# Scores of two slots in one row-tiled visit, in a PSUM tile of five banks

## The chip, the cores and the metric

The kernel runs on one core of one Trainium2 chip. The metric is the device time of one execution in microseconds; the median of several runs counts. All data are fp32.

The engines are named as in the profile: PE (TensorE matmuls) with PEld (its weight loads), DVE (VectorE), ACT (ScalarE), POOL (GpSimd) and SP (the queue that issues most DMAs). PSUM is the memory that matmuls write; it has 8 banks, each with room for 512 fp32 values in each of 128 partitions. A matmul of fp32 shows in the trace as two weight loads and two matmul records.

## What is computed

Threshold attention over 8 batches and 8 heads, sequence 576, head size 64, and then a two-layer MLP with GELU over all 4608 rows:

```python
scores = scale * np.matmul(q, k.transpose(0, 1, 3, 2))          # (8, 8, 576, 576)
thresh = np.max(scores, axis=-1, keepdims=True) - tau
scores = np.where(scores >= thresh, scores, -1000000000.0)
attn = np.exp(scores - np.max(scores, axis=-1, keepdims=True))
attn = attn / (np.sum(attn, axis=-1, keepdims=True) + 1e-09)
x = np.matmul(attn, v)                                          # then rearranged to (4608, 512)
h = x @ w_in                                                    # w_in (512, 2048)
out = (0.5 * h * (1.0 + erf(h / sqrt(2)))) @ w_out              # w_out (2048, 512)
```

## The kernel before

The order of all instructions on each engine is written out by hand; the framework adds the semaphores between engines.

**Pairs and slots.** Two heads form a pair, p = 0 to 31; head e = 0 lies in partitions 0 to 63 of the transposed queries (qT) and keys (kT), head e = 1 in partitions 64 to 127. The 576 query rows of a pair are four chunks of 128 (i = 0 to 3) and one of 64, and the 64 last rows of both heads together make chunk i = 4, which is one tile of 128 rows (q_tail). A slot is one (p, i). The first four pairs (p < EARLY) run while weights are loaded and converted; their slots are in another order and their transposes are made on PE. The 28 others run slot after slot.

**One slot.** `scores` (L394) makes the scores of a slot: for every head two matmuls of 288 columns, each half in a bank of its own. For i < 4 the heads use the upper and the lower 64 rows of the PE array at once (row tiling). The scores of each head are a tile `sc` of two banks, and there are two such buffers, four banks in all. `softmax_head` (L406) takes, head by head, the maximum on DVE (L415), the threshold on POOL (L416) and the exponential on ACT (L418), all but the threshold from `sc`. `softmax_tail` (L421) masks and sums on DVE, head by head (L434), and reads `sc` again. After that `turn_p` (L488) transposes the probabilities on DVE (L498), and DMAs regroup them. In slot 2 `turn_qk` (L375) transposes the next pair's queries and keys on DVE, and `weigh_v` (L522) multiplies the previous pair's probabilities with v into two tiles `xT`.

**MLP beside it.** Eight of the eighteen blocks of 256 rows (PLAIN) run between the slots. `fill` (L637) puts in as many matmuls as a table of goals says; `block_steps` (L602) makes hT = w_in.T x (tiles `hT`, L613), then the second product (tiles `o_ps`, L628). The GELU of a finished hT is put off: `gelus(left)` (L573) leaves `left` of them, 0 at the start of a slot, `lag[0]` within `fill` (2 in the later slots). `table` (L596) brings back the exponential's table on ACT.

**The last stage.** The ten last blocks are multiplied by two levels of a Strassen-Winograd scheme (`last_blocks`, L973). `chain` (L828) makes up to seven products m1 to m7 into three PSUM tiles: x (m1, m6, m5), y (m7, m4, m3) and v (m2). After each product `taken` (L809) copies the tile on ACT or adds it into a sum on DVE. m5 and m3 are made in the following chain: `m1, m5 of the chain before, m7, m2, m3 of the chain before, m6, m4`. `layer_in` (L856) has 7 chains with all seven products, `layer_out` (L920) five single products and then 5 chains without m2; each runs eight times.

**PSUM.** The pool `ps` (L80) has tag `sc` with 2 buffers of two banks and tag `mm` with 4 buffers of one bank, for hT, o_ps, xT, the transposes `tr`, and y and v of the last stage. The lines that matter:

```python
ps = ctx.enter_context(tc.tile_pool(name="ps", bufs=4, space=PSUM))
sc = s["sc", i] = [ps.tile([P, 2, 512], FP32, tag="sc", name="sc", bufs=2) for _ in range(n)]
```

Of the kernel before, what the change touches and what calls it, by code (L numbers as in the profile page):

```python
# [8 lines left out]
FP32 = mybir.dt.float32  # L9
# [9 lines left out]
def kernel(  # L19
# [57 lines left out]
    const = ctx.enter_context(tc.tile_pool(name="const", bufs=1))  # L77
    small = ctx.enter_context(tc.tile_pool(name="small", bufs=4))
    dram = ctx.enter_context(tc.tile_pool(name="dram", bufs=1, space=bass.MemoryType.DRAM))
    ps = ctx.enter_context(tc.tile_pool(name="ps", bufs=4, space=PSUM))  # L80

    XSLOTS = 7
    w_in_all = const.tile([P, N_DM, d_ff], FP32, name="w_in")
# [38 lines left out]
    make_identity(nc, ident)  # L122


    q_tail = [att.tile([P, P], FP32, name=f"q_tail{i}") for i in range(4)]
    v_sb = [att.tile([P, 2, KR, D], FP32, name=f"v{i}") for i in range(4)]

# [173 lines left out]
    def turn_qk_early(p):  # L301


        s = st[p]
        if 2 <= p < HP:
            qT = op.tile([P, MAIN], FP32, tag="o_sb", name="qT")
            kT = pd_tail[p - 2].rearrange("p b i -> p (b i)")
        else:
            qT = ld.tile([P, MAIN], FP32, tag="qT", name="qT")
            kT = ld.tile([P, TAIL + S], FP32, tag="kT", name="kT")  # L310
        s["qT"], s["kT"] = qT, kT
        qt = s["q_tail"] = q_tail[p % 4]
        copy = nc.scalar.copy if p else nc.vector.tensor_copy
        for name in "qk":
            t = s[name]
            tr = ps.tile([P, NC, P], FP32, tag="mm", name="tr")
# [8 lines left out]
        tr = ps.tile([P, NC, P], FP32, tag="mm", name="tr")  # L325
# [12 lines left out]

    def turn_p_early(p, i):


        s = st[p]
        if i == 0 or (p < HP and i == 2):
            s["pT"] = [one.tile([P, KR, S], FP32, tag=f"pT{e}", name=f"pT{e}") for e in range(2)]
        w = s.pop(("p", i))
        n = 1 if i == NC else 2

        def turn(to, at):
            nc.tensor.transpose(to, w[:, at:at + P], ident)  # L349

        for e in range(n):
            tr = ps.tile([P, NC, P], FP32, tag="mm", name="tr")
# [9 lines left out]
        tr = ps.tile([P, NC, P], FP32, tag="mm", name="tr")  # L362
# [12 lines left out]
    def turn_qk(p):  # L375
# [7 lines left out]
        qt = s["q_tail"] = q_tail[p % 4]  # L383
        qs, ks = s.pop("q"), s.pop("k")
        nc.vector.transpose(kT.rearrange("p (b i) -> p b i", i=Q), ks)
        nc.vector.transpose(
            qT.rearrange("p (c a i) -> p c a i", c=NC, i=Q),
            qs[:, 0:MAIN // Q, :].rearrange("p (a c) j -> p c a j", c=NC))
# [3 lines left out]
                qt[rows, e * TAIL:(e + 1) * TAIL].rearrange("p (b i) -> p b i", i=Q), qs[rows, MAIN // Q:NB, :])  # L392

    def scores(p, i):  # L394
        s = st[p]
        n = 1 if i == NC else 2
        sc = s["sc", i] = [ps.tile([P, 2, 512], FP32, tag="sc", name="sc", bufs=2) for _ in range(n)]
        for h in range(2):
            for e in range(n):
                rows = slice(0, P) if i == NC else slice(e * D, (e + 1) * D)  # L400
                lhsT = s["q_tail"] if i == NC else s["qT"][rows, i * P:(i + 1) * P]
                at = h * HALF + (TAIL if p < EARLY and e == 0 else 0)
                nc.tensor.matmul(  # L403
                    sc[e][:, h, 0:HALF], lhsT=lhsT, rhs=s["kT"][rows, at:at + HALF], start=True, stop=True)

    def softmax_head(p, i):  # L406

# [3 lines left out]
        thr = s["thr", i] = small.tile([P, 2], FP32, tag="thr", name="thr")  # L411
        w = s["p", i] = work.tile([P, 2 * S], FP32, tag="p", name="p")
        for e in range(n):
            sc = s["sc", i][e][:, :, 0:HALF]
            nc.vector.tensor_reduce(nmx[:, e:e + 1], sc, axis=AXIS.XY, op=ALU.max, negate=True)  # L415
            nc.gpsimd.tensor_scalar(  # L416
                thr[:, e:e + 1], nmx[:, e:e + 1], -1.0, tau_eff, op0=ALU.mult, op1=ALU.subtract)
            nc.scalar.activation(  # L418
                w[:, e * S:(e + 1) * S].rearrange("p (h s) -> p h s", h=2), sc, AF.Exp, bias=nmx[:, e:e + 1], scale=1.0)

    def softmax_tail(p, i):  # L421

# [7 lines left out]
            at = [e * NC + i if i < NC else 2 * NC for e in range(n)]  # L430
            den = [sums[p % 2][:, x:x + 1] for x in at]
        for e in range(n):
            row = w[:, e * S:(e + 1) * S].rearrange("p (h s) -> p h s", h=2)
            nc.vector.scalar_tensor_tensor(  # L434
                row, sc[e][:, :, 0:HALF], thr[:, e:e + 1], row, op0=ALU.is_ge, op1=ALU.mult, accum_out=den[e])
# [9 lines left out]
    def divide_early(p, lo, hi):  # L445
# [1 line left out]

        s = st[p]
        b, hp = divmod(p, HP)
        tr = ps.tile([P, 512], FP32, tag="mm", name="tr")  # L450
# [348 lines left out]
    def product(to, pairs, start):  # L799
        for k, (l, r) in enumerate(pairs):  # L800
            nc.tensor.matmul(to, lhsT=l, rhs=r, start=start and k == 0, stop=k == len(pairs) - 1,  # L801
                             skip_group_check=not start)

    def bank(tag, n):
        if tag == "sc":
            return ps.tile([P, 2, 512], FP32, tag="sc", name="bank", bufs=2)[:, 0, 0:n]
        return ps.tile([P, 512], FP32, tag="mm", name="bank")[:, 0:n]

    def taken(to, x, first):  # L809

# [208 lines left out]
    nc.scalar.activation(warm[:, 1:2], warm[:, 0:1], AF.Exp)  # L1019
    load_early(1)  # L1020
    load_early(2)
    for t in q_tail + v_sb:
        nc.gpsimd.memset(t, 0.0)
    for _ in range(4):
        load_piece(nc.sync)
# [34 lines left out]
    for n in range(len(slots) + WEIGH + 1):  # L1060
# [69 lines left out]
            turn_qk(p + 1)  # L1130
        convert(0 if n == 0 else 1200 if n < 3 else 2200 if n < BATCH - 1 else 1e9)
        if not early:
            lag[0] = 2 if p < NP else 0
            if n != BATCH:
                fill(owed, tokens)
                owed = 0.0
# [49 lines left out]
```

## Time and profile before

| what | value |
|---|---|
| median of 3 runs | 1352.98 us (1352.51 to 1354.1) |
| profiled execution | 1353.51 us, span 1351.4 us |
| granted PE clock, mean | 0.993 |
| sc matmuls, two heads (L403, 64x128 weights, 288 columns) | 960 + 64 records, 175.6 us busy |
| sc matmuls, last rows (L403, 128x128 weights) | 120 + 8 records |
| maximum on DVE (L415) | 288 x 750 ns, 205.4 us |
| exponential on ACT (L418) | 288 x 738 ns, 201.9 us |
| mask and sum on DVE (L434) | 288 x 816 ns, 225.3 us |
| transpose of probabilities on DVE (L498) | 112 x 1378 ns, 154.4 us |
| hT (L613), o_ps (L628) matmuls | 1024 and 512 records, 241.8 and 236.8 us |
| xT matmuls (L537) | 1280 records, 169.3 us |
| sums of the last stage on DVE (L683, 128x320 and 128x256) | 304 x 488 ns, 240 x 420 ns |

Busy times are sums over the span; several engines are busy at once. The mean of one instruction counts from its start to its end, and matmuls overlap in that sense, so their busy time is less than count times mean. In the profile's groups an arrow `out<-in` gives tiles by the program's names with the buffer numbers left out, and `x288` the count. A wait "A <- B" is idle time of engine A that ended when B's instruction did. In timelines, an entry with x8 merges eight neighbours of one kind.

### The profile page before, as it was taken

Reading aid. Unit: us, or ns where it says so; the run is one execution under the profiler, and the core shown is the slowest. Engines: PE = TensorE matmul, PEld = TensorE weight load, DVE = VectorE, ACT = ScalarE, POOL = GpSimd, SP = SyncE. Lnnn points to the kernel's source line nnn. Section 1 sums busy time; section 2 is a strip of 40 time slices with the busy share of each in tenths; the row PEclk is TensorE's granted clock in tenths of the full one; section 3 lists DMA queues with packets and bytes.
Section 4 is the critical chain, followed back from the end, with each engine's and each line's share of the span. In section 5 each row is a group of like instructions: output and inputs, shape, how many; then the busy total and the mean of one; then the engine's idle time right before and its main releaser. Section 6 shows DMA issues by size and latency. Waiting matters only on the chain.

```text
span 1351.4 us, 19821 instructions
## 1 busy us (share of the span) xinstructions
PE 1323.0 (98%) x6282; PEld 893.8 (66%) x6282; DVE 1048.1 (78%) x1997; ACT 605.0 (45%) x1027; POOL 659.0 (49%) x1097
## 2 busy tenths in 40 slices
PE   8799899999999999999999999999999999999998
PEld 6476557467467557557557557568787787877877
DVE  6987677788888888888888888874758698385765
ACT  7876527548547538537638636413201112211120
POOL 5785354555555554554554551144363513635530
PEclk9899999999999999999999999999999999999999
DMA  8642276677777787687687777500000041000003
GB/s 268 187 151 52 58 164 156 146 162 185 155 180 182 161 193 178 160 207 172 153 208 180 155 179 152 117 9 0 1 0 1 14 112 32 0 1 0 1 0 78
DMA packets 209781, 152.39 MB, mean 113 GB/s; under 512 B 113360, under 2 KB 193088, under 8 KB 209680
## 3 DMA queue, kind: packets, MB, share of 16 engines
q1 hardware_dynamic: 188224, 112.53, 37.5%
q0 software_dynamic: 21024, 38.32, 9.9%
q8 instruction: 51, 0.84, 0.3%
q14 instruction: 50, 0.41, 0.1%
q10 hardware_dynamic: 432, 0.30, 0.1%
HBM read 55.97 MB, written 12.52 MB: 51 GB/s over the span
## 4 chain that ended last, share of the span: by engine, by line
PE 93%; DVE 3%; ACT 3%; DMA 1%; issue 1%; SPq 0%; POOL 0%; DVEq 0%; ACTq 0%; POOLq 0%
PE bank L801 34%; PE o_ps L628 17%; PE hT L613 16%; PE sc L403 14%; PE xT L537 11%; ACT p L418 1%; DMA x<-xall 1%; DVE nmx L415 1%; DVE p L434 1%; PE tr L349 1%; ACT pT L356 1%; DVE power L212 0%; ACT power L202 0%; DVE power L210 0%; PE tr L456 0%
## 5 line engine op out<-in xcount | busy, mean ns | idle before, releaser
L418 ACT ACTIVATE p<-sc,nmx 128x576 f32<-128x576 f32 x288 | 201.9, 738 | 284.0 <-DVE nmx L415 283.7
L434 DVE SCALAR_TENSOR_TENSOR p<-sc,thr,p 128x576 f32<-128x576 f32 x288 | 225.3, 816 | 70.1 <-ACT p L418 68.6
L416 POOL TENSOR_SCALAR thr<-nmx,tau_eff 128x1 f32<-128x1 f32 x288 | 88.0, 307 | 368.0 <-DVE nmx L415 355.8
L415 DVE TENSOR_REDUCE nmx<-sc 128x1 f32<-128x576 f32 x288 | 205.4, 750 | 53.5 <-PE sc L403 52.3
L613 PE MATMUL hT<-xall,w_in 128*128 128x256 f32 x1024 | 241.8, 385 | 0.0
L628 PE MATMUL o_ps<-w_out,g 128*128 128x512 f32 x512 | 236.8, 603 | 0.0
L613 PEld LDWEIGHTS hT<-xall,w_in 128*128 128x128 f32 x1024 | 189.4, 190 | 50.0 <-issue 23.0
L683 DVE TENSOR_TENSOR c<-c,bank 128x320 f32<-128x320 f32 x304 | 147.3, 488 | 33.6 <-PE bank L801 20.1
L683 DVE TENSOR_TENSOR o<-o,bank 128x256 f32<-128x256 f32 x240 | 99.8, 420 | 93.7 <-PE bank L801 88.7
L403 PE MATMUL sc<-kT,qT 64*128 64x288 f32 x960 | 161.8, 431 | 9.3 <-DVE p L434 8.6
L537 PE MATMUL xT<-pT,v 128*64 128x256 f32 (+1 forms) x1280 | 169.3, 418 | 0.8 <-DVE pT L360 0.5
L628 PEld LDWEIGHTS o_ps<-w_out,g 128*128 128x128 f32 x512 | 93.1, 190 | 109.1 <-issue 106.8
L498 DVE STREAM_TRANSPOSE turned_p<-p 128x1152 f32<-128x1152 f32 x112 | 154.4, 1378 | 3.9
L403 PEld LDWEIGHTS sc<-kT,qT 64*128 64x128 f32 x960 | 92.4, 187 | 83.8 <-issue 69.7
L537 PEld LDWEIGHTS xT<-pT,v 128*64 128x64 f32 x1280 | 93.0, 140 | 75.4 <-issue 15.1
L801 PE MATMUL bank<-w_out,c 128*128 128x256 f32 x480 | 120.2, 381 | 0.5 <-DVE o L683 0.5
L269 POOL DMA_DIRECT2D v<-in_v_dram x208 | 110.9, 536 | 3.9 <-issue 1.9
L801 PEld LDWEIGHTS bank<-w_out,c 128*128 128x128 f32 x480 | 89.9, 190 | 18.8 <-DVE o L683 3.0
L854 ACT ACTIVATE c<-c 128x320 f32<-128x320 f32 (+1 forms) x80 | 46.9, 623 | 114.6 <-DVE c L683 114.6
L683 POOL TENSOR_TENSOR c<-c,g 128x320 f32<-128x320 f32 (+1 forms) x40 | 50.5, 1271 | 67.4 <-DVE c L683 67.4
L801 PE MATMUL bank<-t_out,c 128*128 128x256 f32 x320 | 82.7, 381 | 0.0
L801 PE MATMUL bank<-t_out,g 128*128 128x256 f32 x320 | 82.1, 379 | 0.0
(179 smaller groups left out, 1775.1 us busy)
## 6 DMA issues: line engine op xcount, KB each, us to landing
pT<-turned_p SPq DMA_DIRECT2D x448, 160.0 KB, 3.6
pT<-pd_tail SPq DMA_DIRECT2D x112, 80.0 KB, 3.0
q<-in_q_dram POOLq DMA_DIRECT2D x104, 72.0 KB, 3.4
k<-in_k_dram POOLq DMA_DIRECT2D x104, 72.0 KB, 3.2
inv<-turned SPq DMA_DIRECT2D x54, 128.0 KB, 3.9
v<-in_v_dram POOLq DMA_DIRECT2D x156, 40.0 KB, 3.1
out_dram<-o SPq DMA_DIRECT2D x40, 128.0 KB, 2.4
xall<-in_moe_w_out_dram POOLq DMA_DIRECT2D x9, 512.0 KB, 3.8
```

Of the source, the lines that this page charges most:

```text
L269: eng.dma_start(t[r:P:4, e, 0:n, :], rows[:, r * KR:r * KR + n, :])
L403: nc.tensor.matmul(sc[e][:, h, 0:HALF], lhsT=lhsT, rhs=s["kT"][rows, at:at + HALF], start=True, stop=True)
L415: nc.vector.tensor_reduce(nmx[:, e:e + 1], sc, axis=AXIS.XY, op=ALU.max, negate=True)
L416: nc.gpsimd.tensor_scalar(thr[:, e:e + 1], nmx[:, e:e + 1], -1.0, tau_eff, op0=ALU.mult, op1=ALU.subtract)
L418: nc.scalar.activation(w[:, e * S:(e + 1) * S].rearrange("p (h s) -> p h s", h=2), sc, AF.Exp, bias=nmx[:, e:e + 1], scale=1.0)
L434: nc.vector.scalar_tensor_tensor(row, sc[e][:, :, 0:HALF], thr[:, e:e + 1], row, op0=ALU.is_ge, op1=ALU.mult, accum_out=den[e])
L498: nc.vector.transpose(turned_p[:, :, i // 2, 0:NB, i % 2 * Q:(i % 2 + 1) * Q], w.rearrange("p (e b i) -> p e b i", e=2, i=Q))
L537: nc.tensor.matmul(to, lhsT=s["v"][:, e, c, :], rhs=rhs, start=(c == 0), stop=(c == KR - 1))
L613: nc.tensor.matmul(hT[:, j % 2, :], lhsT=w_in_sb[c][:, j * P:(j + 1) * P], rhs=x_blk[n][:, c, :], start=(c == 0), stop=(c == N_DM - 1))
L628: nc.tensor.matmul(o[:, 0:d_model], lhsT=g[j][:, m * P:(m + 1) * P], rhs=w_out_sb[j], start=(j == 0), stop=(j == N_DF - 1))
L683: eng.tensor_tensor(out, a, b, op=ALU.add)
L801: nc.tensor.matmul(to, lhsT=l, rhs=r, start=start and k == 0, stop=k == len(pairs) - 1, skip_group_check=not start)
```

## The change

The scores lie in one PSUM tile `sc_all` of five banks. Two slots have a place in it at the same time: slot "pair" 0 has head 0 at columns 0 to 575 and head 1 at 1408 to 1983, "pair" 1 has head 0 at 576 to 1151 and head 1 at 1984 to 2559. Each region crosses one border of banks, so each head's scores are two matmuls of unequal size (512 + 64, 128 + 448, 448 + 128, 64 + 512 columns).

In the 28 later pairs `scores` makes slots 0 and 1 in one visit, 2 and 3 in one, and slot 4 alone; `flip` alternates which slot takes which place. Both row tiles would write bank 2 in such a visit, so the 128 last columns of place 1, head 0 are made first by a matmul over all 128 rows, with both heads' qT as weights and `k_end` as the other operand: the keys of head 0 with zeros for head 1. `turn_qk` copies `k_end` on ACT.

The pool of `mm` has three buffers instead of four. The early transposes and spread tiles take bank 4 of `sc_all` every fourth time, as long as no later slot uses it (`spare_bank`). In the last stage `bank` puts x in banks 0 and 1 of `sc_all` in turn, and y and v in turn in the `mm` pool and in banks 2 to 4. Maximum, exponential and mask read one run of 576 columns instead of two of 288. `lag[0]` in the later slots is 1 instead of 2.

```diff
-    ps = ctx.enter_context(tc.tile_pool(name="ps", bufs=4, space=PSUM))
+    ps = ctx.enter_context(tc.tile_pool(name="ps", bufs=3, space=PSUM))
+    BANK = 512
+    sc_all = ps.tile([P, 5 * BANK], FP32, tag="sc", name="sc", bufs=1)
+    SC_AT = {(0, 0): 0, (1, 0): S, (0, 1): 5 * BANK - 2 * S, (1, 1): 5 * BANK - S}
+    flip = [0]
+    CUT = 2 * BANK - S
+    spare = [0]
+    def spare_bank():
+        spare[0] = (spare[0] + 1) % 4
+        if spare[0] or (EARLY in st and ("sc", 1) in st[EARLY]):
+            return ps.tile([P, BANK], FP32, tag="mm", name="tr")
+        return sc_all[:, 4 * BANK:5 * BANK]
...
+    k_end = att.tile([P, 2 * S - 2 * 512], FP32, name="k_end")
...
+        nc.scalar.copy(k_end[0:D, :], kT[0:D, CUT:S])
...
     def scores(p, i):
         s = st[p]
-        n = 1 if i == NC else 2
-        sc = s["sc", i] = [ps.tile([P, 2, 512], FP32, tag="sc", name="sc", bufs=2) for _ in range(n)]
-        for h in range(2):
-            for e in range(n):
-                rows = slice(0, P) if i == NC else slice(e * D, (e + 1) * D)
-                lhsT = s["q_tail"] if i == NC else s["qT"][rows, i * P:(i + 1) * P]
-                at = h * HALF + (TAIL if p < EARLY and e == 0 else 0)
-                nc.tensor.matmul(
-                    sc[e][:, h, 0:HALF], lhsT=lhsT, rhs=s["kT"][rows, at:at + HALF], start=True, stop=True)
+        if p >= EARLY and i < NC and i % 2:
+            return
+        first = flip[0] if p >= EARLY else 0
+        todo = [i, i + 1] if p >= EARLY and i < NC else [i]
+        parts = []
+        for k, c in enumerate(todo):
+            pair = (first + k) % 2
+            heads = range(1 if c == NC else 2)
+            s["sc", c] = [sc_all[:, SC_AT[pair, e]:SC_AT[pair, e] + S] for e in heads]
+            for e in heads:
+                cut = -SC_AT[pair, e] % BANK or BANK
+                start = 0
+                for lo, hi in (0, cut), (cut, S):
+                    whole = c < NC and pair == 1 and e == 0 and lo == CUT
+                    parts.append((-1 if whole else k, start, e, c, lo, hi))
+                    start += hi - lo
+        for k, _, e, c, lo, hi in sorted(parts):
+            rows = slice(0, P) if c == NC or k < 0 else slice(e * D, (e + 1) * D)
+            lhsT = s["q_tail"] if c == NC else s["qT"][rows, c * P:(c + 1) * P]
+            at = TAIL if p < EARLY and e == 0 else 0
+            rhs = k_end if k < 0 else s["kT"][rows, at + lo:at + hi]
+            nc.tensor.matmul(s["sc", c][e][:, lo:hi], lhsT=lhsT, rhs=rhs, start=True, stop=True)
+        if i == NC and p >= EARLY:
+            flip[0] ^= 1
...
+    turn = {"sc": 0, "mm": 0}
     def bank(tag, n):
-        if tag == "sc":
-            return ps.tile([P, 2, 512], FP32, tag="sc", name="bank", bufs=2)[:, 0, 0:n]
-        return ps.tile([P, 512], FP32, tag="mm", name="bank")[:, 0:n]
+        turn[tag] += 1
+        k = turn[tag] % (2 if tag == "sc" else 6)
+        if tag == "mm" and k % 2:
+            return ps.tile([P, BANK], FP32, tag="mm", name="bank")[:, 0:n]
+        k = k if tag == "sc" else 2 + k // 2
+        return sc_all[:, k * BANK:k * BANK + n]
...
-            lag[0] = 2 if p < NP else 0
+            lag[0] = 1 if p < NP else 0
```

More of the change, by code (lines that the diff above doesn't have):

```diff
@@ L315, in turn_qk_early @@
             t = s[name]
-            tr = ps.tile([P, NC, P], FP32, tag="mm", name="tr")
+            tr = spare_bank().rearrange("p (c s) -> p c s", s=P)
             for c in range(NC):
@@ L324, in turn_qk_early @@
                 copy(kT[:, TAIL:S], src)
-        tr = ps.tile([P, NC, P], FP32, tag="mm", name="tr")
+        tr = spare_bank().rearrange("p (c s) -> p c s", s=P)
         for j, name in enumerate("qk"):
@@ L351, in turn_p_early @@
         for e in range(n):
-            tr = ps.tile([P, NC, P], FP32, tag="mm", name="tr")
+            tr = spare_bank().rearrange("p (c s) -> p c s", s=P)
             for c in range(NC):
@@ L361, in turn_p_early @@
         tails = s["pT"][0][:, NC, :]
-        tr = ps.tile([P, NC, P], FP32, tag="mm", name="tr")
+        tr = spare_bank().rearrange("p (c s) -> p c s", s=P)
         turn(tr[:, 0, :], MAIN if i < NC else S - P)
@@ L413, in softmax_head @@
         for e in range(n):
-            sc = s["sc", i][e][:, :, 0:HALF]
-            nc.vector.tensor_reduce(nmx[:, e:e + 1], sc, axis=AXIS.XY, op=ALU.max, negate=True)
+            sc = s["sc", i][e]
+            nc.vector.tensor_reduce(nmx[:, e:e + 1], sc, axis=AXIS.X, op=ALU.max, negate=True)
             nc.gpsimd.tensor_scalar(
@@ L418, in softmax_head @@
             nc.scalar.activation(
-                w[:, e * S:(e + 1) * S].rearrange("p (h s) -> p h s", h=2), sc, AF.Exp, bias=nmx[:, e:e + 1], scale=1.0)
+                w[:, e * S:(e + 1) * S], sc, AF.Exp, bias=nmx[:, e:e + 1], scale=1.0)
     def softmax_tail(p, i):
@@ L432, in softmax_tail @@
         for e in range(n):
-            row = w[:, e * S:(e + 1) * S].rearrange("p (h s) -> p h s", h=2)
+            row = w[:, e * S:(e + 1) * S]
             nc.vector.scalar_tensor_tensor(
-                row, sc[e][:, :, 0:HALF], thr[:, e:e + 1], row, op0=ALU.is_ge, op1=ALU.mult, accum_out=den[e])
+                row, sc[e], thr[:, e:e + 1], row, op0=ALU.is_ge, op1=ALU.mult, accum_out=den[e])
         if p < EARLY:
@@ L449, in divide_early @@
         b, hp = divmod(p, HP)
-        tr = ps.tile([P, 512], FP32, tag="mm", name="tr")
+        tr = spare_bank()
         for i in range(lo // P, -(-hi // P)):
@@ L1021 @@
     load_early(2)
-    for t in q_tail + v_sb:
+    for t in q_tail + v_sb + [k_end]:
         nc.gpsimd.memset(t, 0.0)
```

## The prediction

> **What bounds the kernel now.** I read the page's engine shares and chain first, then busy time by stage, then who waits for whom in the attention stage, then the timelines of single slots.
>
> ```profile
> PE 1323.0 (98%) x6282; PEld 893.8 (66%) x6282; DVE 1048.1 (78%) x1997; ACT 605.0 (45%) x1027; POOL 659.0 (49%) x1097
> PE 93%; DVE 3%; ACT 3%; DMA 1%; issue 1%; SPq 0%; POOL 0%; DVEq 0%; ACTq 0%; POOLq 0%
> ```
>
> TensorE holds 93% of the chain that ended last. By stage (columns: stretch, its length, then busy us of PE, PEld, DVE, ACT, POOL):
>
> ```profile
> 0.00:138.60 138.60, 120.93 (x814) 87.92 (x815) 104.24 (x205) 102.41 (x210) 91.90 (x146) 0.95 0.55 161
> 138.60:862.00 723.40, 717.54 (x3470) 433.13 (x3471) 608.11 (x1089) 408.49 (x624) 367.59 (x759) 1.00 0.73 165
> 862.00:900.00 38.00, 38.00 (x130) 19.58 (x129) 30.48 (x62) 7.53 (x16) 12.25 (x16) 1.00 0.27 61
> 900.00:1351.00 451.00, 446.52 (x1872) 353.20 (x1871) 305.29 (x644) 86.61 (x178) 187.30 (x176) 1.00 0.07 18
> ```
>
> The second stretch is the 28 later head pairs, 723.4 / 28 = 25.84 us each; VectorE is 84% busy there, so it has little room. The waits of 200 to 860 us (total, times, longest):
>
> ```profile
> DVE p L434 <- ACT p L418: 57.2, 127, 2.5
> DVE nmx L415 <- PE sc L403: 31.1, 54, 2.2
> PE sc L403 <- DVE p L434: 1.6, 2, 1.3
> ```
>
> TensorE loses 1.6 us there to buffers of scores. A one-head slot, then a two-head slot:
>
> ```profile
> 505.25 0.76 DVE L415 TENSOR_REDUCE nmx<-sc 128x1 f32<-128x576 f32 x1
> 506.04 0.74 ACT L418 ACTIVATE p<-sc,nmx 128x576 f32<-128x576 f32 x1 [3.23 <-DVE nmx L415]
> 506.88 0.82 DVE L434 SCALAR_TENSOR_TENSOR p<-sc,thr,p 128x576 f32<-128x576 f32 x1 [0.88 <-ACT p L418]
> ...
> 512.64 1.24 PE L403 MATMUL sc<-kT,qT 64*128 64x288 f32 x8
> 513.81 3.72 PE L613 MATMUL hT<-xall,w_in 128*128 128x256 f32 x16
> ...
> 513.91 1.42 DVE L415 TENSOR_REDUCE nmx<-sc 128x1 f32<-128x576 f32 x2
> 514.79 1.35 ACT L418 ACTIVATE p<-sc,nmx 128x576 f32<-128x576 f32 x2
> 515.62 0.82 DVE L434 SCALAR_TENSOR_TENSOR p<-sc,thr,p 128x576 f32<-128x576 f32 x1 [0.28 <-ACT p L418]
> ```
>
> In a two-head slot head 0's exponential lies beside head 1's maximum: maxima 1.42 together, and from the first maximum to the end of the second mask (517.18) 3.27 us. The one-head slot shows the serial price: maximum to mask 1.63 us. Finally the last stage:
>
> ```profile
> 1012.30 0.70 PE L801 MATMUL bank<-x,s_out 128*128 128x320 f32 x2
> 1012.84 0.70 PE L801 MATMUL bank<-t_x,s_out 128*128 128x320 f32 x2
> ...
> 1012.50 0.49 DVE L683 TENSOR_TENSOR g<-g,bank 128x320 f32<-128x320 f32 x1
> ```
>
> A product takes 0.54 us; the sum that empties it starts 0.2 us after it, lasts 0.49, and runs beside the next products, because each product has a bank tile of its own.
>
> **What the skill says.** "PSUM — Partial Sum Buffer", section on bank collisions: two engines may not be at one bank and quadrant together, and the compiler back end adds a dependency between them, "reads and writes alike". No run here shows a collision; the trace's overlaps are all on different banks. "TensorEngine Tiling (Array Packing)", Key Properties: a change of tiling mode drains TensorE; Gotcha 1: row tiles may not write one bank together. The trace agrees on the first: eight score matmuls stream in about 0.97 us (four steps of 0.243), and hT starts 1.17 after them, with some 0.2 more lost on entry; I take 0.4 us for both switches.
>
> **The premise that decides.** What waits for what is set by the framework that places the semaphores. From small programs built with it: for an SBUF tile it follows regions, but for a PSUM tile it follows the whole tile and lets one engine at it at a time, readers too, even where banks differ. Today two heads' scores, and every product of the last stage, are tiles of their own. The change makes one tile, sc_all, of five banks, for four score regions, a quarter of the early transposes and most accumulators of the last stage. No page states a whole-tile rule and the trace of before cannot show it; the bank rule is the rival below.
>
> **Attention stage, by the premise.** Head 1's maximum waits for head 0's exponential and head 0's mask for head 1's exponential. From first maximum to last mask: 1.63 + 1.63 + 1.56 (both masks, 515.62 to 517.18) = 4.82 instead of 3.27. A visit of TensorE may begin only when the last mask is done and no maximum before the whole visit is done. The visit: 0.1 signal, 0.11 weight load, 0.22 for the full-row piece (two records of 128 columns), 0.2 switch, 2.05 for head 1's pieces (128, 448, 64, 512 columns, two records each, at 0.84 ns a column from hT's 0.215 us per 256, short ones at 0.107, the price of a 128-column weight load in "TensorE: Matmul & The Clock Gate", LDWEIGHTS), 0.19 to the first maximum: 2.87. Slot by slot:
> - slot 0: 4.82 + 0.04 + the transpose of 1.38 (L498) = 6.24
> - slot 1: 4.82 + the visit 2.87 (the transpose lies beside it) = 7.69
> - slot 2: 4.82 + 0.04 + 3.04 (transpose and turn_qk, 522.56 to 525.60) = 7.90
> - slot 3: 4.82 + the one-head visit, full mode, 0.1 + 0.11 + 1.03 + 0.19 = 6.25
> - slot 4: 2.45 (505.25 to 507.70) + 2.87 = 5.32
>
> Sum 33.4 against 25.84: +7.56, times 28 = **+212 us**. TensorE's 24.7 us a pair fit inside, so mode switches saved are worth nothing here. For the same reason three banks instead of four, lag 1 instead of 2 and the k_end copy (64 x 128 on ScalarE, an estimated 0.27 us behind turn_qk's transpose) cost nothing; in the rival where TensorE still bounds they do.
>
> **Early stage.** 16 two-head slots with +1.55 = 25 us; 19 of the 76 early transposed or spread tiles go to bank 4 of sc_all, so TensorE waits for the exponentials and the mask for ScalarE's copy: 1 us each as a middle value (0 to 2), 19. Uneven pieces, 512 + 64 beside 128 + 448: 0.1 each, hidden. **+45** (15 to 75).
>
> **Last stage.** x is always in sc_all; of the others every second one. Where two products on sc_all follow each other, the second waits: 0.2 + 0.49 + 0.06 signal + 0.11 weight load = 0.86 us (0.79 with 256 columns, whose sum takes 0.42); with one other product of 0.54 between, 0.32 is left; with one of 0.86, nothing. The 56 chains of layer_in: one direct and three covered, 0.86 + 0.96 = 1.82, 102 us. The 40 of layer_out: three of five have both accumulators in sc_all (four direct, 3.16), two one (1.58), and v some 1.6 a round: 8 x (3 x 3.16 + 2 x 1.58 + 1.6) = 114. **+216** (150 to 260). That six banks for y and v now stand where four did could win back at most the 4.5 us for which a weight load waits for VectorE.
>
> **Clock.** TensorE would idle some 4 us twice a pair. "TensorE: Matmul & The Clock Gate", Part 1, has the clock halved after an idle window of about 3.4 us; the profile before shows a lower clock only in its first slices (0.95 over 138.6 us). An estimate: a quarter of 56 gaps, 1 us each: **+14** (0 to 60).
>
> **Sum.** The profiled execution took 1353.51 (span 1351.4 and 2.1 around it): 1353.5 + 212 + 45 + 216 + 14 = 1840.5. The median of the runs is 0.5 lower; I forecast 1840.
>
> **Rivals.**
> *Waits by bank, TensorE and VectorE in step.* For: the column layout, built so that heads of one slot share no bank. Then heads overlap as now, but slots share banks 1 to 3, so a visit starts late and the maximum waits for most of it. Worked as above: of six borders in two pairs, three leave VectorE idle for 1.1, 0.7 and 1.1 us; 1.45 a pair, 41 us. Besides, with three banks handed out in order of release the second xT of slot 2 gets the bank of slot 1's hT, whose GELU stands behind slot 2's exponentials (ends 523.41, xT begins about 521.4); some 1.3 us in 13 pairs, partly in the same gaps. About 1400.
> *Faster.* If no read of sc_all waits for another read, and slot 2's regions are free well before TensorE comes, it stays bound by its own work: 56 visits fewer x 0.4 = -22.4; full-row pieces 56 x 0.22 = +12.1; short pieces 56 x 0.1 = +5.6; tails and early pieces +3; last stage -4.5. About 1347. It decides from where VectorE's part of two slots (9 to 10 us) is shorter than TensorE's work up to the next visit (6.9 us from slot 1, so against it).
>
> **How the numbers follow.** Whole-tile waits 0.84, by bank 0.10, faster 0.06. The first case with its bounds gives 1700 to 1970, which holds nearly all of its chance; the others are left out. About 0.2% (2.7 us) is what can be told from no change. The rivals' own spread gives faster 0.05, same 0.02, slower 0.93.
>
> **What would show it.** Right: DVE nmx <- ACT p appears as a large wait in a slot (some 0.9 us per two-head slot); ACT and DVE never at sc together; TensorE near 72% busy; PE bank <- DVE and ACT in the last stage about 200 us; a pair every 33 us. Wrong: the two maxima still within 1.42 us, or last-stage products still 0.54 apart; then waits go by bank or region and a rival holds. Pair period right but last stage too short would mean covered waits there.

## The result and the profile after

The changed kernel takes 1998.64 us (median of 4 runs, 1993.83 to 2002.43) against 1352.82 before: a ratio of 1.477, 95% interval 1.4735 to 1.4804. The forecast of 1840 us had the direction and the kind of loss, and was 159 us short. The profiled execution took 1993.83 us, its span is 1992.1.

One statement about the kernel before has to be put right first, because the largest miss hangs on it. The section on it gives x the products m1, m6, m5 and y the products m7, m4, m3. The last line of `chain` says otherwise, in both kernels:

```python
waiting.append((one_of("m5", x, False), one_of("m3", x, False)))
```

x takes four products (m1, m6, m5 and m3), y two (m7 and m4).

Engine shares and chain of the changed kernel:

```profile
PE 1534.4 (77%) x6282; PEld 916.8 (46%) x6282; DVE 1055.7 (53%) x1997; ACT 634.5 (32%) x1059; POOL 658.3 (33%) x1098
PE 42%; DVE 29%; ACT 10%; SPq 7%; issue 6%; DMA 5%; POOL 0%; DVEq 0%; ACTq 0%; POOLq 0%
```

Before, TensorE alone was 93% of the chain. Now the chain changes engine all the time and no engine is full: a sign of waits, not of work. By stage (the columns of the same view before: length, busy time of PE, PEld, DVE, ACT, POOL, granted clock, DMA share, GB/s):

```profile
0.00:192.30 192.30, 133.38 (x822) 96.47 (x823) 95.56 (x204) 105.62 (x211) 92.88 (x147) 0.87 0.39 116
192.30:1187.30 995.00, 800.60 (x3462) 482.81 (x3463) 618.19 (x1089) 432.68 (x655) 367.26 (x759) 0.91 0.53 120
1187.30:1222.00 34.70, 33.26 (x109) 15.08 (x107) 27.50 (x54) 6.11 (x13) 9.23 (x13) 1.00 0.31 71
1222.00:1992.00 770.00, 567.12 (x1892) 322.48 (x1892) 314.45 (x650) 90.10 (x181) 188.92 (x180) 1.00 0.04 11
```

The number of instructions of each stage is nearly what it was. VectorE's busy time grew by 2% in the attention stage and by 3% in the last; the stages grew by 38% and 71%. In numbers: early 138.6 to 192.3 (+53.7), attention 723.4 to 995.0 (+271.6), the short stretch -3.3, the last stage 451 to 770 (+319). One more thing stands in the clock column: 0.91 in the attention stage, where it was 1.00.

Who waits for whom, 200 to 1187 us (total, times, longest):

```profile
PE sc L434 <- DVE p L466: 162.4, 56, 7.3
DVE nmx L447 <- PE sc L434: 147.9, 63, 7.6
DVE p L466 <- ACT p L450: 112.1, 127, 1.2
DVE nmx L447 <- ACT p L450: 96.4, 111, 3.4
```

The first line was 1.6 us before, and the last was not among the leading waits. TensorE waits for the mask, then VectorE waits for TensorE: they take turns. The border between slots 1 and 2 of one pair shows it:

```profile
596.53 0.72 DVE L447 TENSOR_REDUCE nmx<-sc 128x1 f32<-128x576 f32 x1
597.28 0.74 ACT L450 ACTIVATE p<-sc,nmx 128x576 f32<-128x576 f32 x1 [3.76 <-DVE nmx L447]
598.06 0.76 DVE L447 TENSOR_REDUCE nmx<-sc 128x1 f32<-128x576 f32 x1 [0.81 <-ACT p L450]
598.85 0.74 ACT L450 ACTIVATE p<-sc,nmx 128x576 f32<-128x576 f32 x1 [0.82 <-DVE nmx L447]
599.69 0.82 DVE L466 SCALAR_TENSOR_TENSOR p<-sc,thr,p 128x576 f32<-128x576 f32 x1 [0.88 <-ACT p L450]
600.43 0.81 DVE L466 SCALAR_TENSOR_TENSOR p<-sc,thr,p 128x576 f32<-128x576 f32 x1
601.31 0.49 PE L434 MATMUL sc<-k_end,qT 128*128 128x128 f32 x2 [3.42 <-DVE p L466]
601.73 3.75 PE L434 MATMUL sc<-kT,qT 64*128 64x448 f32 x14
605.53 0.76 DVE L447 TENSOR_REDUCE nmx<-sc 128x1 f32<-128x576 f32 x1 [2.86 <-PE sc L434]
```

Head 1's maximum starts only after head 0's exponential, although the two heads' scores share no bank; before, the two maxima ran back to back in 1.42 us. First maximum to last mask is 4.71 us here, and 4.72 to 4.76 us by the median of each two-head slot (forecast 4.82). TensorE starts when the last mask is done, and the next maximum when the whole visit is done. The visit here takes 4.28 us instead of the forecast 2.87. And in the last stage, products of one chain:

```profile
1450.76 0.81 PE L833 MATMUL sc<-xall,s_out 128*128 128x320 f32 x2
1451.61 0.49 DVE L715 TENSOR_TENSOR c<-c,sc 128x320 f32<-128x320 f32 x1 [0.36 <-PE sc L833]
1452.15 0.81 PE L833 MATMUL sc<-t_x,s_plain 128*128 128x320 f32 x2 [0.58 <-DVE c L715]
1452.99 0.49 DVE L715 TENSOR_TENSOR c<-c,sc 128x320 f32<-128x320 f32 x1 [0.90 <-PE sc L833]
1453.54 0.81 PE L833 MATMUL sc<-x,s_in 128*128 128x320 f32 x2 [0.58 <-DVE c L715]
```

Products stand 1.39 us apart instead of 0.54, each waiting for the sum that empties its predecessor. That is the forecast price (0.54 + 0.86 = 1.40), but here three products on sc_all follow each other, and the forecast had counted fewer such neighbours.

### The profile page after: what moved, and what is told of

It reads as the page before. It is cut to its first block, busy times and chain, and to the rows that moved or that the text cites. A ratio compares the mean times of both kernels' runs of the same rounds, so it can differ in the third digit from the quotient of the medians.

```text
span 1992.1 us, 19527 instructions
## 1 busy us (share of the span) xinstructions
PE 1534.4 (77%) x6282; PEld 916.8 (46%) x6282; DVE 1055.7 (53%) x1997; ACT 634.5 (32%) x1059; POOL 658.3 (33%) x1098
## 4 chain that ended last, share of the span: by engine, by line
PE 42%; DVE 29%; ACT 10%; SPq 7%; issue 6%; DMA 5%; POOL 0%; DVEq 0%; ACTq 0%; POOLq 0%
PE sc L833 23%; PE sc L434 9%; DVE p L466 7%; DVE nmx L447 7%; ACT p L450 7%; SPq L552 6%; PE bank L833 4%; DVE c L715 4%; DVE o L715 4%; DVE turned_p L530 3%; DMA pT<-pd_tail 3%; PE o_ps L660 2%; PE hT L645 2%; PE xT L569 2%; DMA pT<-turned_p 1%
## 5 line engine op out<-in xcount | busy, mean ns | idle before, releaser
L447 DVE TENSOR_REDUCE nmx<-sc 128x1 f32<-128x576 f32 x288 | 217.1, 754 | 273.4 <-PE sc L434 162.0
L569 PE MATMUL xT<-pT,v 128*64 128x256 f32 (+1 forms) x1280 | 183.8, 438 | 31.5 <-ACT g L618 31.5
L715 DVE TENSOR_TENSOR o<-o,sc 128x256 f32<-128x256 f32 x194 | 81.7, 421 | 213.5 <-PE sc L833 211.3
L434 PE MATMUL sc<-kT,qT 64*128 64x512 f32 (+2 forms) x848 | 184.6, 561 | 13.1 <-DVE p L466 12.1
L715 DVE TENSOR_TENSOR c<-c,sc 128x320 f32<-128x320 f32 x216 | 105.4, 488 | 152.1 <-PE sc L833 152.1
L434 PEld LDWEIGHTS sc<-kT,qT 64*128 64x128 f32 x848 | 108.8, 231 | 50.6 <-issue 24.2
L833 PE MATMUL sc<-w_out,c 128*128 128x256 f32 x384 | 104.4, 394 | 35.7 <-DVE c L715 18.6
L833 PE MATMUL sc<-t_out,g 128*128 128x256 f32 x320 | 90.5, 405 | 42.0 <-DVE o L715 33.5
L434 PE MATMUL sc<-k_end,qT 128*128 128x128 f32 x112 | 29.0, 345 | 100.2 <-DVE p L466 100.2
L833 PEld LDWEIGHTS sc<-w_out,c 128*128 128x128 f32 x384 | 67.8, 189 | 68.2 <-DVE c L715 30.3
```

Source lines behind the costliest of these rows:

```text
L434: nc.tensor.matmul(s["sc", c][e][:, lo:hi], lhsT=lhsT, rhs=rhs, start=True, stop=True)
L447: nc.vector.tensor_reduce(nmx[:, e:e + 1], sc, axis=AXIS.X, op=ALU.max, negate=True)
L569: nc.tensor.matmul(to, lhsT=s["v"][:, e, c, :], rhs=rhs, start=(c == 0), stop=(c == KR - 1))
L715: eng.tensor_tensor(out, a, b, op=ALU.add)
```

## The experiments

Two readings stood against each other throughout: that a PSUM tile is waited for as a whole, readers included, or that waits go by bank. Below that lay the sizes: why the last stage lost 319 us and not 216, and why slot 1 took 9.26 us and not 7.69.

**One tile for both heads, and nothing else.** The kernel before, with one line changed in `scores`; the last stage keeps a bank tile for every product, from a pool of its own (that part of the edit is not shown).

```diff
-        sc = s["sc", i] = [ps.tile([P, 2, 512], FP32, tag="sc", name="sc", bufs=2) for _ in range(n)]
+        both = ps.tile([P, 4, 512], FP32, tag="sc", name="sc", bufs=1)
+        sc = s["sc", i] = [both[:, 2 * e:2 * e + 2, :] for e in range(n)]
```

> The kernel before with one edit: both heads' scores of a slot lie in one tile of four banks instead of two tiles of two banks each; every address pattern, bank, visit and lag stays, and the last stage keeps a bank tile for every product. Theory (a PSUM tile is waited for as a whole, readers too): head 1's maximum waits for head 0's exponential, first maximum to last mask goes from 3.2 to 4.8 us, slots take about 6.4, 6.4, 7.9, 6.3 and 4.0 us, a pair about 31 us instead of 25.84, the attention stage +143 us, the early stage +25, last stage 451: about 1520 us (1480 to 1560). Rival (waits by bank): no bank is shared, so nothing changes: 1353 us.

Measured 1518.01 us in one run (before, beside it: 1353.05). A two-head slot of this kernel in the timeline, and its attention and last stage by windows:

```profile
505.36 0.76 DVE L417 TENSOR_REDUCE nmx<-sc 128x1 f32<-128x576 f32 x1
506.34 0.73 ACT L420 ACTIVATE p<-sc,nmx 128x576 f32<-128x576 f32 x1
507.10 0.76 DVE L417 TENSOR_REDUCE nmx<-sc 128x1 f32<-128x576 f32 x1 [0.98 <-ACT p L420]
...
510.44 1.24 PE L405 MATMUL sc<-kT,qT 64*128 64x288 f32 x8 [1.47 <-DVE p L436]
```

```profile
156.00:1025.60 869.60, 734.16 (x3471) 437.95 (x3471) 621.52 (x1089) 417.83 (x624) 367.97 (x759) 0.98 0.62 138
1064.00:1515.00 451.00, 447.01 (x1874) 353.56 (x1872) 305.56 (x645) 86.87 (x178) 187.30 (x176) 1.00 0.07 18
```

No matmul, shape or order differs from the kernel before, and the two heads still share no bank. Yet the second maximum waits for the first exponential, and TensorE for the last mask. 869.6 / 28 = 31.06 us a pair, +146 us in the stage; +17 in the early stage. Waits by bank could not hold the second maximum back. TensorE's wait for the last mask would not decide by itself, because one tile now stands where two took turns; that TensorE, too, waits across banks is seen in the last stage, next. The rule of the whole tile is shown, and so is the price of the two waits together.

**The last stage's tiles given back.** The changed kernel; `ps` is closed ahead of the last stage, and `bank` takes from a new pool.

```diff
...
-        k = k if tag == "sc" else 2 + k // 2
-        return sc_all[:, k * BANK:k * BANK + n]
+        return tail["ps"].tile([P, 512], FP32, tag=tag, name="bank", bufs=2 if tag == "sc" else 6)[:, 0:n]
```

> The changed kernel with one edit: in the last stage x, y and v get bank tiles of their own again (two for sc, six for mm) in place of bank-wide pieces of sc_all. Theory (whatever shares one PSUM tile waits for it as a whole): the stalls between neighbouring products go, the last stage falls from 770 us to 451 to 456 as before the change, the attention stage stays at 995 us, and the time is about 1999 - 317 = 1682 us (1670 to 1695). Rival (waits go by bank, and the last stage is long for another reason, such as the order of the products or three banks in the pool): the last stage stays near 770 us and the time near 1999.

Measured 1687.35 us in one run. By windows, the attention stage and the last:

```profile
193.80:1195.30 1001.50, 808.88 (x3462) 488.17 (x3463) 617.70 (x1089) 433.52 (x655) 368.03 (x759) 0.90 0.53 119
1230.00:1685.00 455.00, 450.70 (x1888) 356.21 (x1886) 307.46 (x649) 88.09 (x181) 190.09 (x180) 1.00 0.07 18
```

The last stage is back at 455 us. Of the 319 us that the stage had lost, 315 came from sharing the tile. The products have the same number of banks in both kernels, and by the code products that follow each other on sc_all lie in different banks of it, so waits by bank would not have held them.

**m3 on y.** This puts the layout on the chip that the forecast had counted.

```diff
-        waiting.append((one_of("m5", x, False), one_of("m3", x, False)))
+        waiting.append((one_of("m5", x, False), one_of("m3", y, False)))
```

> The changed kernel with one name changed: in chain, m3 is multiplied into y instead of x, which changes what is computed (m3 is then added to m7 + m4, not to m1 + m6 + m5) but no number of instructions. Theory (the last stage is too long against the forecast only because m3 follows m6 on the same x in sc_all, so that some 340 products follow a direct neighbour on sc_all and not some 200): the last stage falls from 770 us by about 110 to 660 (640 to 685) and the time to about 1890. Rival (the price of a neighbour or something else in the stage was mis-sized, the order does not matter): the stage stays within 20 us of 770 and the time at 1980 to 2000.

Measured 1900.36 us; from the first product of the last stage to the last it is 674 us, and 770 in the changed kernel. From the start times of the 672 products, the time between a product and the next, less the 0.54 or 0.86 us of the product itself:

```
product -> next                    changed kernel    m3 on y
sc 320  -> sc 320                  145 x 0.85 us      49 x 0.87 us
sc 256  -> sc 256                  154 x 0.76        122 x 0.75
sc      -> sc, other width          44 x 0.90         36 x 0.94
other 320 -> sc 320                104 x 0.20        152 x 0.20
sc 320  -> other 320               105 x 0.10        153 x 0.10
all pauses                         318 us            222 us
```

The prices hardly move, the number of direct neighbours falls from 343 to 207, and with it the loss falls to 222 us. The forecast's term was 216. So its price per neighbour was right and its count was that of another program.

**No early transpose in sc_all.** `if spare[0] or (...)` in `spare_bank` becomes `if True`.

> The changed kernel with one edit: the early transposes never go to bank 4 of sc_all, always to a bank of the pool. Theory (a transpose in sc_all waits for the exponentials and the mask of the scores that stand in the same tile): 19 transposes lose about 1 us each, so the early stage falls from 192 us to about 173 (157 to 187) and the time to about 1980. Rival (the early stage is longer by the slot's serial chain alone, or three pool banks are what it lacks): no change or slower, 1999 to 2010 us.

Measured 1969.51 us, 29 less than the changed kernel; the early stage is 165.3 us instead of 192.3. In the changed kernel's early stage TensorE's leading waits are these; the last three, transposes into sc_all held by readers of scores, are gone without the shared bank:

```profile
PE sc L434 <- DVE p L466: 32.4, 17, 3.2
PE sc L334 <- ACT p L450: 7.0, 2, 3.8
PE sc L364 <- ACT p L450: 4.9, 2, 2.6
PE sc L364 <- DVE p L466: 4.1, 2, 2.5
```

Those three make 16 us, and the scores behind them wait less too (the first line falls to 19.0 us). In all it is 27 us, 1.4 for each of the 19 transposes, where the forecast had 1.

**The long visit, first try.** Four matmuls of 128x512 at the end of slot 1, in a bank of their own that nobody reads, to keep TensorE busy up to the visit:

```diff
+        if EARLY <= p < NP and i == 1:
+            warmer = ps.tile([P, BANK], FP32, tag="mm", name="warmer")
+            for _ in range(4):
+                nc.tensor.matmul(warmer, lhsT=ident, rhs=w_in_sb[0][:, 0:BANK], start=True, stop=True)
```

> The changed kernel with four matmuls of 128x512 added at the end of slot 1 of the later pairs; they write a bank that nobody reads and only keep TensorE busy in the gap before the visit of slots 2 and 3. Theory (the visit of slots 2 and 3 is long because the granted clock has fallen to about 0.66 after 3.5 to 4 us without work): the visit goes from 4.3 to 5.3 us back to about 2.9, slot 1 from 9.26 to about 7.7 us, 28 times 1.5 = 44 us less: about 1955 us (1945 to 1970). Rival (the visit is long because of its many short pieces or the switch of tiling mode): slot 1 stays at 9.3 us or grows by what the extra matmuls take, 1999 to 2020 us.

Measured 2028.27 us: slower than the changed kernel by 30, which neither side expected. Slot 1 falls in two groups: 7.6 us in 14 of 26 pairs, but 11.3 to 14.3 in 10. The waits say why:

```profile
PE warmer L1177 <- ACT g L618: 40.4, 11, 4.1
```

In those pairs the next bank of the pool was still to be emptied by a GELU, and the added matmuls, and the visit behind them, waited for it. The bank that the added matmuls took brought a wait of its own, so the time decides nothing; the 14 short slots alone speak for the clock.

**The long visit, second try.** The same four matmuls ahead of the first real product of the first hT or o_ps tile that slot 1 takes, in that same tile:

```diff
                     hT = ps.tile([P, 2, TOK], FP32, tag="mm", name="hT")
+                    warmer(hT.rearrange("p a b -> p (a b)"))
...
                     o = ps.tile([P, 512], FP32, tag="mm", name="o_ps")
+                    warmer(o)
```

> The changed kernel with four matmuls of 128x512 whose result is overwritten, put ahead of the first product of the first hT or o_ps tile that slot 1 of a later pair takes, in that tile, so that no further bank is taken (the kernel with the warmer bank took one and waited for ScalarE's GELU). Theory (TensorE's granted clock falls in the gap before the visit of slots 2 and 3, and with the gap filled the visit is 2.9 us): slot 1 is 7.6 us in nearly every pair instead of 9.26, and the time falls by up to 28 x 1.6 = 45 us: about 1960 (1950 to 1980). Rival (the visit is long because of its pieces): slot 1 stays above 9 us and the time at 1995 to 2030.

Measured 1981.52 us, ratio 1.4649 (1.4619 to 1.4679), 17 less. A visit that meets a warm TensorE, in the timeline of this kernel:

```profile
531.26 3.60 PE L638 MATMUL hT<-w_in,ident 128*128 128x512 f32 x8
534.69 0.59 PE L653 MATMUL hT<-xall,w_in 128*128 128x256 f32 x2
536.13 0.49 PE L434 MATMUL sc<-k_end,qT 128*128 128x128 f32 x2 [0.84 <-DVE p L466]
536.55 2.33 PE L434 MATMUL sc<-kT,qT 64*128 64x448 f32 x14
```

The same 14 records take 2.33 us, and 3.75 in the timeline of the changed kernel above. Over 26 pairs (the 28 later ones without the first and the last, as in all means of slots here), the time from the last mask of slot 1 to the next maximum, against how long TensorE had stood idle at that mask:

```
idle before the visit   changed kernel              gap filled
under 1 us              none                        15 x 2.85 to 2.86, 2 x 3.9
1 to 3 us               2.86, 2.86, 3.82, 4.00      2.86, 4.53
over 3 us               22 x, 4.13 to 5.27          7 x, 3.89 to 5.27
```

(The two of 3.9 had no gap: the work ran on past the mask, and the visit began 1.2 us after it.) Pieces and switches are the same in every row, and the clock goes with the length: over these stretches of the changed kernel the mean granted clock is 1.00 where they last 2.86 us, 0.62 to 0.72 at 3.8 to 4.6 us and 0.50 to 0.52 at 5.2 to 5.3 us. The visit's length is the clock's doing. That the time fell by 17 us and not by 45 has two reasons. In nine pairs the gap stayed, whole or in part. And of the 30 us that slot 1 gave up (28 x 1.07), slots 3 and 4 took back 14 (28 x 0.51): in the pair looked at, the shifted products made xT later, and ScalarE's copy of xT stood ahead of slot 3's first exponential, which began 2.0 us after the start of its maximum and not 0.75 as in the slot shown first.

After slot 4, too, the next maximum comes late in ten of the 26 pairs of the changed kernel, 3.4 to 4.7 us after the mask. There it is not the visit that is long:

```profile
653.86 4.40 PE L660 MATMUL o_ps<-w_out,g 128*128 128x512 f32 x6
655.75 0.82 DVE L466 SCALAR_TENSOR_TENSOR p<-sc,thr,p 128x576 f32<-128x576 f32 x1 [0.88 <-ACT p L450]
658.10 0.38 PE L434 MATMUL sc<-k_end,qT 128*128 128x128 f32 x2
658.41 2.33 PE L434 MATMUL sc<-kT,qT 64*128 64x448 f32 x14
```

The mask is done at 656.57, but TensorE is still at the products put into slot 4, and the visit begins 1.5 us later; it then takes its usual 2.33 us for the 14 records. In all ten pairs the granted clock in slot 4 up to the mask is 0.50 to 0.71, and the visit begins 0.7 to 2.0 us after the mask. In the other sixteen the clock there is 1.00. So in slot 4 the lowered clock, which follows an idle stretch in slot 3, costs its time in the products ahead of the visit.

**Three banks by themselves.** The kernel before, its pool at `bufs=3` and `lag[0] = 1`.

> The kernel before with three PSUM banks instead of four for the other matmuls in every stage and lag 1 instead of 2; scores as before, in tiles of their own. Theory (with three banks handed out in order of release, slot 2's second xT gets the bank of slot 1's hT, whose GELU stands behind slot 2's exponentials): TensorE waits about 2 us in some 13 pairs and a little more in the early stage, 1365 to 1395 us, best guess 1380. Rival (the wait is covered by work that TensorE has to spare): within 5 us of 1353.

Measured 1392.26 us, ratio 1.0292 (1.0276 to 1.0308): +39 us. The attention stage takes 29 us of it (slot 2 is 7.93 us instead of 6.92), the early stage 9. Bank count and lag change together here; a lag of 1 with four banks was not run. TensorE's waits for banks in this kernel:

```profile
PE xT L537 <- ACT g L586: 20.1, 12, 1.9
PE tr L349 <- ACT pT L356: 6.3, 11, 0.7
```

The wait that the rival by bank had put into 13 pairs is real in 12 of them, 1.7 us each. It is not hidden in a kernel that TensorE bounds.

**One-slot visits in sc_all.** The changed kernel with `todo = [i]`, every slot with its own visit. In this kernel slot 3 of every second pair takes its 128 last columns of head 0 from the next pair's keys, because turn_qk has written k_end anew by then; the work is the same.

> The changed kernel with one-slot visits: every slot's scores are made in a visit of their own again, still in sc_all and its column layout, with three banks in the pool, lag 1 and k_end. Theory (the attention stage lost 146 us to one tile for both heads and the other 125 to the visit of two slots, which begins only when both slots are done and meets a lowered clock after slot 1): slots 1 and 4 fall from 9.26 and 5.73 us to about 6.2 and 4.0, a pair from 35.5 to about 31, the attention stage from 995 us to 868 (860 to 885), the time to about 1872. Rival (the 125 us belong to the three banks, the uneven pieces or k_end): slots 1 and 4 stay long and the time is above 1950.

Measured 1928.76 us: a gain of 70 us where 127 were expected. Slots 1 and 4 fell as expected (6.39 and 4.16 us), but slot 2 rose from 7.85 to 9.70. Two waits of TensorE explain it:

```profile
PE xT L567 <- ACT g L616: 27.8, 13, 2.4
PE sc L432 <- ACT k_end L401: 20.4, 10, 6.2
```

The second goes when every piece is taken from kT, row-tiled (`whole = False`):

> The kernel with one-slot visits in sc_all, and no full-row piece: every piece goes row-tiled from kT, k_end is copied but not read. In the run before, slot 2 took 9.7 us, because a visit of slot 3 comes after turn_qk and waited for k_end's copy behind the transposes. Theory (that wait alone was the excess): slot 2 falls to about 7.9 us, slots 0 and 1 to 6.2, a pair to about 31 us, the attention stage to about 870 us, the time to about 1872 (1860 to 1885). Rival (three banks in the pool, or the uneven pieces, cost what is left): slot 2 stays at 9 to 10 us and the time at 1900 to 1930.

Measured 1902.63 us (1897.9 to 1907.35), slot 2 still 9.40 us: the rival. The first line is left (28.2 us in this kernel), and it is the three banks again. Slots 0 and 1 take 6.27 and 6.19 us, so nothing is seen of a price of uneven pieces.

**Only the tile left.** The last two kernels once more, each also with the last stage's own tiles and no early transpose in sc_all.

> The changed kernel with three parts undone together: one-slot visits, the last stage's tiles of their own, no early transpose in sc_all. Left are the one tile of five banks for both heads, three banks in the pool, lag 1 and k_end. Theory (the parts add, and three banks and the k_end copy are covered while the slots' chain bounds): 1999 - 127 - 313 - 28 = about 1530 (1515 to 1545), some 10 us above the kernel before with one tile for both heads (1518). Rival (the parts overlap, or three banks cost here what they cost in the kernel before, 39 us): 1550 to 1580.

> As the run just named, with the last stage's tiles of their own and no early transpose in sc_all. Left of the change are the one tile of five banks for both heads, three banks in the pool, lag 1 and an unread k_end. Theory (the parts add, and three banks are covered while the slots' chain bounds): about 1872 - 313 - 28 = 1531 (1515 to 1545), some 10 us above the kernel before with one tile for both heads (1518). Rival (three banks cost here too what they cost in the kernel before, 39 us): 1550 to 1575.

Measured 1590.09 us, above either side's range, with both waits just named in it; and 1560.78 without the full-row piece, which is the rival's. A slot 2 of the latter:

```profile
480.41 0.60 ACT L617 ACTIVATE g<-hT 128x512 f32<-128x512 f32 x1
...
481.06 4.14 PE L568 MATMUL xT<-pT,v 128*64 128x256 f32 x20 [2.27 <-ACT g L617]
...
485.75 1.29 PE L433 MATMUL sc<-kT,qT 64*128 64x512 f32 x8
...
487.08 0.76 DVE L446 TENSOR_REDUCE nmx<-sc 128x1 f32<-128x576 f32 x1 [3.28 <-PE sc L433]
```

The last mask was done at 480.76. The second xT waits until the GELU has given its bank back, and slot 3's scores stand behind xT on TensorE; a slot that should end at about 483.9 ends at 487.08: 2.27 us are the wait, and xT then took 4.14 us at a granted clock of 0.59, where the xT at 475.88 had taken 2.91 us at 1.00. Against the kernel before with one tile for both heads, slot 2 is longer by 9.36 - 7.90 = 1.46 us, 41 us in 28 pairs (the stage by 34, as slots 3 and 4 are a little shorter).

**Six banks in the last stage of the kernel before.** As in the second experiment, without the rest.

> The kernel before with six bank tiles instead of four for y and v in the last stage (two for x as before). The stage has 2.7 us of pauses between its products, so theory: at most 2.7 us less, 1350 to 1353. Rival: the change of the pool at the stage's start makes TensorE wait for the last banks of the attention stage: 1353 to 1360.

Measured 1354.5 us, ratio 1.001 (1.0002 to 1.0018): no gain. None of the kernels tried is faster than the one before.

From before to after in one line, by medians: 1353, one tile for both heads 1518 (+165), three banks with the rest of the layout 1561 (+43), early transposes and last stage in sc_all 1903 (+342), two-slot visits with their full-row piece 1999 (+96).

## Why the prediction was right in kind and short in size

- **Premise, whole-tile waits: right**, shown by the one-line edit (+146 us in the attention stage, +143 expected). Both rivals with waits by bank or region are out.
- **Slots.** Forecast 6.24, 7.69, 7.90, 6.25, 5.32 us; measured mean 6.13, 9.26, 7.85, 6.36, 5.73. Slots 0, 2 and 3 agree to 0.11 us. The chain of 4.82 is 4.72 to 4.76. The visit of 2.87 is 2.84 to 2.86 wherever TensorE was at full clock and free when the mask was done: in slot 4 in 16 of 26 pairs of the changed kernel, in slot 1 in only two.
- **Clock: mis-sized.** The term was "a quarter of 56 gaps, 1 us each", 14 us. In slot 1 it was 24 of 26 visits, and the slot was 1.57 us longer on average than forecast: 44 us. In slot 4 the clock slowed the products ahead of the visit in ten of 26 pairs, 1.1 us each: 11 us. That makes 55 us where 14 stood. A gap of 4 us was in the forecast, but that only a quarter of the gaps would count was worked out from nothing. A visit wholly at half clock is 2.46 us of streaming twice and 0.4 around it, 5.3 us; the longest measured are 5.27.
- **Last stage: the step that failed.** "The 56 chains of layer_in: one direct and three covered" and "three of five have both accumulators in sc_all (four direct, 3.16), two one" rest on m3 going to y. With m3 on x (v in sc_all and y in the pool, as in the forecast's own count), a layer_in chain has three direct neighbours and two covered: 3 x 0.86 + 2 x 0.32 = 3.22 us, 180 for 56. In layer_out it is six direct or two: 8 x (3 x 6 x 0.79 + 2 x 2 x 0.79 + 1.6) = 152. Together 332; measured 318 between products and 319 for the stage. The unit prices stood: 0.86 and 0.79 forecast, 0.85 and 0.76 measured; one product between, 0.32 forecast, 0.20 and another 0.10 ahead of the product in between. The count was 343 and not about 200, and putting m3 where the forecast had it gives back 96 of the 103 us.
- **Early stage:** 45 forecast, 54 measured; the part of the transposes was 27 and not 19. The other 27 look like the 25 forecast for the slots, but that is in part luck: one tile for both heads cost 17 by itself (first experiment), and three banks cost 9 in the kernel before, a term that the forecast put at nothing.
- **Three banks, lag 1 and the k_end copy at no cost: right for the attention stage of this kernel, for an incomplete reason.** It was put down to TensorE's room. But the kernels with one-slot visits have room too, and the last of them lost 41 us in slot 2 to the same wait for the GELU and the lowered clock after it. What covers it in the changed kernel is that slot 3's scores are already made when xT waits: slot 2 is 7.8 us in 25 of 26 pairs. A wait on a half-idle engine is free only if what stands behind it on that engine is not needed next.
- **Sum.** 1840, with last stage +103, attention +60, early +9, the short stretch -3, the separate clock term -14 (it is inside the stages now), and 5 for the profiled execution against the median: 2000, measured 1998.64. The range ended at 1970 because it took the clock and the neighbours' price as what was uncertain, and the count as known.

Left open: how the price of three banks divides between the bank and the lag. Two-slot visits with a tile for each head were not tried: two tiles of three banks leave two banks for everything else.

## What to carry to other kernels

A PSUM tile is the unit of waiting in this framework, so before joining tiles list every engine that touches them and ask who may no longer overlap, two readers included. "Perfetto Trace Analysis" in the Trainium skill (Optimizing Tensor Performance, Matmuls) advises that "independent matmul groups should rotate through different PSUM banks"; here groups in different banks of one tile took turns all the same, at 0.76 to 0.85 us each, and with tiles of their own the stage took 455 us instead of 770. And a loss that is a price times a count deserves as much care for the count: read the order of the accumulators off the line that queues them, since one letter there was worth 98 us.

## What the runs showed of the hardware

The granted clock punishes short waits beyond their length. Around the visit shown first, by windows of the changed kernel (clock in the third column from the end):

```profile
590.00:596.00 6.00, 6.00 (x24) 4.29 (x23) 3.85 (x7) 1.55 (x3) 0.58 (x2) 1.00 0.89 182
601.00:606.00 5.00, 4.69 (x20) 2.93 (x22) 2.10 (x4) 2.65 (x4) 1.83 (x3) 0.66 0.19 45
```

After 3.4 us without a matmul the next five microseconds run at 0.66 of the full clock on average. "TensorE: Matmul & The Clock Gate" in the Trainium skill (Part 1, What's actually happening) has the activity window free-running, so that the moment of the change depends on where in the window the work lands. The trace's record of the clock shows it: the clock is 1.0 or 0.5, and it changes only on a grid of 3.41 us that runs through the whole kernel. Take every stretch of that grid at full clock in the changed kernel, and how much of it TensorE was busy. Where that was 40% or less, the next stretch ran at half clock, in all 43 cases; where it was over 50%, the clock stayed full, in all 461; in between it fell in 5 cases and stayed in 8. Over all fourteen traces it is 338 of 338 and 6034 of 6045. The page's table has the clock fall after an idle window of about 3.4 us. The length agrees, but the stretch need not be idle, and there the measurement decides.

So it matters how a gap lies on the grid. At about 2 us of idle time two of the changed kernel's four visits of slot 1 were long and two short; over 3 us all 22 were long, but anywhere from 4.13 to 5.27. In slot 3 TensorE stood idle for over 3 us in eleven pairs, and in three of them the clock stayed full: there the gap lay across two stretches of the grid, each still busy for 45 to 58%. Where such a wait can't be removed, even useless matmuls ahead of it paid: 17 us net in this kernel.
